# Attention and highway feed-forward on one core: later tail loads, a late last v load, turns ahead of stores

## The chip, the cores and the metric

The kernel runs on one core of one Trainium2 chip. The metric is the device time of one execution in microseconds, the median over several runs. Before the change three runs took 267.73, 270.59 and 270.0 us, so the median is 270.0 us.

## What is computed

For 8 batches of 12 heads, 448 rows and 64 columns, q and k are normalised row by row, the scores are divided by tau = 0.1, and softmax attention over v follows. The heads of a row are then laid side by side (768 numbers) and a highway layer closes the program.

```python
q_n = q / (np.linalg.norm(q, axis=-1, keepdims=True) + 1e-06)
k_n = k / (np.linalg.norm(k, axis=-1, keepdims=True) + 1e-06)
scores = np.matmul(q_n, k_n.transpose(0, 1, 3, 2)) / tau
attn = softmax(scores)
x = np.matmul(attn, v).transpose(0, 2, 1, 3).reshape(B * S, H * D)
H = np.maximum(x @ w_h, 0.0)
T = 1.0 / (1.0 + np.exp(-(x @ w_t + b_t)))
out = T * H + (1.0 - T) * x
```

## The kernel before

The 12 heads of a batch are worked as 6 pairs, so there are 48 pairs, numbered s = 6 b + p. Of the 448 rows of a head 384 form three full blocks of 128, and 64 are the tail. The main rows are loaded by POOL's queue, which turns float32 into float16 on the way: one transfer each for q, k and v of a batch (`ld6 qr b`, `ld6 kr b`, `ld6 vr b`, 576 KB, L342 and L365). The tails stay float32 and come on SP's queue, two transfers of 96 KB for each of q, k and v (`ldqt b h` at L357, `ldkt b ab` at L361, `ldvt b ab` at L367).

From the loads a batch goes through these steps:

- Squares of q and k, summed to norms: `sq3` for the main rows, `sqt b 0` for the q tail (ACT) and `sqt b 1` for the k tail (DVE or ACT), all through L258 or L264, then the folds (L421, L425, L427).
- Seven small DVE steps make the inverse roots (`nt84 b`, L465 to L471).
- The normalised main rows of a pair are written by `qn s` and `kn s` (L258) on DVE or POOL. The normalised tails of a whole batch are written into one buffer by `kb b 0`, `kb b 1` (k) and `qtn b` (q).
- Turning: for batches 4 to 7 SP issues a DMA transpose for each pair (`xd6 q s`, L572, tile qT) and one for the tails of a batch (`xd9 t b`, L599, tile tT). For batches 1 to 6 the rows x that attention leaves are also turned by two DMA transposes of SP (`xd12 b 0` and `xd9 b 1`, L757, tile xT).
- PE makes the scores of a pair in three groups `qk s c` (L642) and one for the tail keys `qkt s` (L657). ACT takes the exponential of each (`exp s c`, L648, and `expt s`, L661).
- PE multiplies with v (`av s c`, L690 and L694, `avt s`, L710), DVE divides by the sums (`rc s`, L718, and `ev s`, L720). v itself is copied beforehand into a buffer with columns of ones (`vc b p` and `vtc b ab`, L261).
- The highway layer of a batch is four groups g = 4 b + i. PE makes `fft`, `ffc` (L800, L807, L791), ACT a tanh (`th`, L848, L849), DVE the relu minus x (`hm`, L867), the gate (`gt`, L872; `gg`, L879) and, with POOL, the sum (`out`, L884). SP stores the rows (`st g` at L898, `sth g h` at L891).

Nothing schedules this at run time. The program is recorded as a list of 1717 operations, and the table `ORDER` gives the order in which they are emitted; every engine then runs its own operations strictly in that order, and a wait of one holds up all behind it. The table `SLOTS` gives, in the order of first use, which buffer of its ring each tile takes:

```python
def follow(self, order, slots):
    out, at = [], 0
    for n in order:
        o = self.ops[n]
        for t in self.new(o):
            self.slot[t] = slots[at]
            at += 1
        out.append(o)
```

The rings that matter here: qt, kt and vt have two buffers each, so batches 4 and 6 share one and 5 and 7 the other; vr has three, vp two; qT three (two pairs each), qn two (two pairs each); PSUM has three double banks `pS` for scores and highway products, and two single banks `pB`. The first highway product of group 13 (`fft4 13 0 0`) takes the bank of `qk 24 1`, so it cannot begin before `exp 24 1` has read it.

The edits touch operations 1303 to 1306 and 1310 (order of k, q and v tails of batch 6), 1505 to 1515 and 1540 to 1545 (those of batch 7 and what hangs on its v), and a few stores and turns, all of them by their place in the table alone.

Of the kernel before, what the change touches and what calls it, by code (L numbers as in the profile page):

```python
# [93 lines left out]
001000101001011010001001001101200002010102110111002010110010120120101112011200001100210200010111101211100200011  # L94
010121101110012010001110200001001021200211101012020101011010201110110121100211010001102011120112012121110000101
100021101121211010022102010100101020101012011210211201110120121001020201210110020012110220201001111102111010011
012001102000110023200021110200121101110010012110121010210102210000201001000112011010203210111001102010110021110
201210221101220100000001111210001102221120101021010210121001021011001110121001110123101211022001101020020100112
201101000120122101120201010102001010110220011012020001102010211111010202120100211120011122111012120012100110211
000200021110010011001010202112221011000010120001001101210001101010221101220201130110201020012020011110100221020  # L100
21032102101100121011102301000121210121010230201
""".replace("\n", "")
)
# [906 lines left out]
```

## Time and profile before

| what | us |
|---|---|
| median of three runs | 270.0 |
| lowest, highest run | 267.73, 270.59 |
| the profiled execution | 272.19 |
| its span, first to last instruction | 270.4 |
| PE busy in the span | 244.4 |
| DVE busy | 228.5 |
| ACT busy | 206.0 |
| POOL busy | 115.9 |

The profiled execution is 1.8 us longer than its span, and 2.2 us longer than the median. "PE" is TensorE, "SPq" the queue of SyncE on which DMAs are issued. In a timeline a row has its start, its length, engine, source line, operation and tiles; what stands in brackets is the idle time of that engine just before the row and what ended it. Rows of SP and DMA rows of POOL are issues: how long the transfer itself takes is told by its landing.

### The profile page before, as it was taken

The page shows a single profiled execution, that of the slowest core. Times are in us where ns is not written, and L with a number is a line of the kernel's source. Part 1 is how long each engine was busy: PE and PEld are TensorE (multiplying, and loading weights), DVE is VectorE, ACT ScalarE, POOL GpSimd, SP SyncE. Part 2 cuts the span into 40 slices and gives each one's busy share as a digit, 9 for nine tenths or more (in the row PEclk, how much of TensorE's full clock was granted, in tenths as well). Part 3 has the DMA queues.
Part 4 walks back from the last instruction along what each step waited for, and adds up shares of the span by engine and source line. Part 5 has one row for each costly group of instructions (what it writes and reads, how often), then busy time and mean ns, then how long its engine had stood idle before and what let it go on. Part 6 is the DMA issues. An engine that isn't in the chain of part 4 may idle for free.

```text
span 270.4 us, 9033 instructions
## 1 busy us (share of the span) xinstructions
PE 244.4 (90%) x3755; PEld 165.0 (61%) x3755; DVE 228.5 (85%) x513; ACT 206.0 (76%) x279; POOL 115.9 (43%) x151
## 2 busy tenths in 40 slices
PE   7088978999999999999899799997999999999991
PEld 3044666676776676667466557664767667767650
DVE  6599899999999898998976978997987864569894
ACT  3379999799999989989589499867868797961120
POOL 8757458563455649335450626314404522002140
PEclk9659999999999999999999799999999999999998
DMA  7999999999899797999999976999939949413133
GB/s 136 207 192 183 179 200 211 194 184 193 136 136 252 103 152 84 172 253 157 178 166 173 187 196 128 206 136 154 235 107 175 183 72 238 80 58 119 63 100 132
DMA packets 104025, 43.32 MB, mean 160 GB/s; under 512 B 97584, under 2 KB 101040, under 8 KB 103984
## 3 DMA queue, kind: packets, MB, share of 16 engines
q0 software_dynamic: 38608, 16.52, 49.1%
q1 hardware_dynamic: 63920, 25.50, 48.8%
q10 hardware_dynamic: 1456, 0.72, 1.0%
q8 instruction: 29, 0.48, 0.7%
q14 instruction: 12, 0.10, 0.1%
HBM read 38.21 MB, written 11.01 MB: 182 GB/s over the span
## 4 chain that ended last, share of the span: by engine, by line
PE 62%; DVE 20%; DMA 7%; issue 4%; ACT 3%; POOL 2%; SPq 1%; DVEq 0%; PEldq 0%; ACTq 0%; POOLq 0%
PE pS L807 26%; PE pS L642 9%; PE pB L694 8%; PE pS L791 4%; PE pB L710 4%; PE pB L657 3%; PE pB L690 3%; DMA kt<-in_k_dram 3%; DVE qn L258 3%; PE pB L582 2%; DMA qr<-in_q_dram 2%; DVE x L720 2%; DMA qT<-qn 2%; DVE f L421 2%; DVE hm L867 1%
## 5 line engine op out<-in xcount | busy, mean ns | idle before, releaser
L648 ACT ACTIVATE E<-pS 128x896 f16<-128x896 f32 x144 | 127.3, 924 | 26.2 <-PE pS L642 22.5
L807 PEld LDWEIGHTS <-xT 64*128 64x128 f16 x1128 | 53.8, 94 | 31.6 <-issue 2.6
L807 PE MATMUL pS<-wt,xT 64*128 64x384 f16 x576 | 56.6, 325 | 0.2 <-PEq L800 0.2
L807 PE MATMUL pS<-wh,xT 64*128 64x384 f16 x552 | 55.7, 323 | 0.2 <-DVE hm L867 0.2
L642 PE MATMUL pS<-qT 64*128 64x384 f16 x288 | 43.9, 332 | 2.3 <-DMA qT<-qn 1.8
L694 PE MATMUL pB<-vp,E 128*128 128x65 f16 x864 | 43.8, 194 | 0.0
L694 PEld LDWEIGHTS <-E 128*128 128x128 f16 x864 | 38.8, 98 | 2.6 <-issue 2.5
L867 DVE SCALAR_TENSOR_TENSOR hm<-pS,x 128x768 f16<-128x768 f32 (+1 forms) x33 | 27.3, 831 | 10.7 <-ACT tt L848 5.7
L642 PEld LDWEIGHTS <-qT 64*128 64x128 f16 x576 | 22.9, 95 | 19.6 <-issue 4.4
L690 PE MATMUL pB<-vp,Et 128*128 128x130 f16 x144 | 32.0, 222 | 2.3 <-DVE x L720 1.9
L258 POOL TENSOR_TENSOR qn<-kr,rs 128x384 f16<-128x384 f16 x24 | 19.8, 827 | 32.9 <-issue 10.0
L884 POOL TENSOR_TENSOR os<-x,hm 128x768 f32<-128x768 f16 (+1 forms) x11 | 15.8, 1441 | 37.7 <-DVE hm L879 17.3
L720 DVE SCALAR_TENSOR_TENSOR x<-pB,rd 128x448 f16<-128x448 f32 x48 | 29.7, 621 | 1.1
L661 ACT ACTIVATE Et<-pB 128x512 f16<-128x512 f32 x48 | 28.9, 609 | 0.9 <-PE pB L657 0.8
L642 PE MATMUL pS<-tT,qT 64*128 64x64 f16 x282 | 27.6, 190 | 0.0
L258 POOL TENSOR_TENSOR qn<-qr,rs 128x384 f16<-128x384 f16 x17 | 14.4, 850 | 14.0 <-DMA qT<-qn 5.6
L884 DVE TENSOR_TENSOR os<-x,hm 128x768 f32<-128x768 f16 (+1 forms) x22 | 18.5, 842 | 0.8 <-POOL os L884 0.6
L845 ACT ACTIVATE tt<-os 128x768 f16<-128x768 f32 (+1 forms) x8 | 6.1, 764 | 17.1 <-DVE os L839 10.0
L710 PE MATMUL pB<-vp,E 128*128 128x65 f16 x288 | 18.6, 195 | 0.5 <-POOL vp L261 0.5
L258 DVE TENSOR_TENSOR qn<-qr,rs 128x384 f16<-128x384 f16 x30 | 17.2, 577 | 0.5 <-POOL qn L258 0.4
L690 PEld LDWEIGHTS <-Et 128*128 128x128 f16 x144 | 14.1, 98 | 5.5 <-issue 4.3
L879 DVE TENSOR_TENSOR hm<-tt,hm 128x768 f16<-128x768 f16 (+1 forms) x33 | 16.4, 503 | 0.4
(116 smaller groups left out, 451.2 us busy)
## 6 DMA issues: line engine op xcount, KB each, us to landing
out_dram<-os SPq DMA_DIRECT2D x23, 384.0 KB, 3.0
vr<-in_v_dram POOLq DMA_DIRECT2D x8, 576.0 KB, 11.3
kr<-in_k_dram POOLq DMA_DIRECT2D x7, 576.0 KB, 10.8
qr<-in_q_dram POOLq DMA_DIRECT2D x7, 576.0 KB, 10.7
qt<-in_q_dram SPq DMA_DIRECT2D x16, 96.0 KB, 5.4
vt<-in_v_dram SPq DMA_DIRECT2D x16, 96.0 KB, 5.6
out_dram<-os SPq DMA_DIRECT2D x15, 96.0 KB, 2.7
kt<-in_k_dram SPq DMA_DIRECT2D x14, 96.0 KB, 6.7
```

Source lines behind the costliest of these rows:

```text
L258: return (nc.vector if eng == "DVE" else nc.gpsimd).tensor_mul(out_, a, c)
L642: ins = nc.tensor.matmul(dst, lhsT=qT[ln, 384 + 128 * c : 512 + 128 * c], rhs=rhs, start=True, stop=True)
L648: return nc.scalar.activation(R("E", s)[:, c, :, 0:448], R("S", 3 * s + c)[:, :, 0:448], AF.Exp, scale=inv_tau)
L661: op("ACT", f"expt {s}", lambda: nc.scalar.activation(R("Et", s)[:, 64:576], R("B", ("S", s))[:, :], AF.Exp, scale=inv_tau), key + 3, r=[( ...
L690: nc.tensor.matmul(U[:, 2 * c : 2 * c + 2, :].rearrange("p g e -> p (g e)"), lhsT=Et[:, 128 + 128 * c : 256 + 128 * c], rhs=vp[:, 6:8, :]. ...
L694: ins = nc.tensor.matmul(U[:, 2 * c + ab, :], lhsT=EF[:, j, 576 * ab + 128 * c : 576 * ab + 128 * c + 128], rhs=vp[:, 3 * ab + j, :], star ...
L710: ins = nc.tensor.matmul(U[:, 6, :], lhsT=lt, rhs=rh, start=(n == 0), stop=(n == 7))
L720: op("DVE", f"ev {s}", lambda: nc.vector.scalar_tensor_tensor(out=R("x", b)[:, :, D * p : D * p + D], in0=U_()[:, :, 0:D], scalar=0.0, in1 ...
L807: ins = nc.tensor.matmul(P[:, h, 0:MH], lhsT=lt, rhs=rh, start=(part == 0 and cc == (-1 if wi == 0 and not added else 0)), stop=(part == 1 ...
L867: return nc.vector.scalar_tensor_tensor(out=o_, in0=i0, scalar=0.0, in1=xs, op0=ALU.max, op1=ALU.subtract)
L879: op("DVE", f"gg{'h' if tail or last_ else ''} {nm}", lambda cs=cs: nc.vector.tensor_mul(R("hm", g)[:, cs], R("tt", g)[:, cs], R("hm", g)[ ...
L884: op(en, f"out{'h' if tail or last_ else ''} {nm}", lambda eng=eng, cs=cs: eng.tensor_add(R("os", g)[:, cs], xall()[:, cs], R("hm", g)[:, ...
```

## The change

Only the two tables change. On SP the k tails of batch 6 move up to where one of the q tails of batch 6 was, and the q tails move down to where the k tails were; the tails of batch 7 and the v tails of batch 6 are gathered at other places; three DMA transposes move ahead of stores. On POOL the v load of batch 7 moves down by some 25 operations. The v copies of batch 7 move with it, and the v buffers of batches 6 and 7 trade places.

```diff
-814 783 483 994 838 484 836 839 834 659 1123 837 974 805 1303 804 787 1310 835 803 976 802 788 660 934 806 832
-817 807 661 833 1029 935 662 818 474 819 663 843 1304 841 820 842 1114 840 1311 485 823 937 824 475 821 650 822
...
+814 783 483 994 838 484 836 839 834 659 1123 837 974 805 804 787 1310 835 803 976 802 788 660 934 806 832 817
+807 661 833 1029 935 1306 1305 662 818 474 819 663 843 841 820 842 1114 840 1311 485 823 937 824 475 821 650
```

First place, SP, the turns of pairs 26 and 27 and of the tails of batch 4. Here qt_76 and kt_78 are the buffers of batches 4 and 6, qt_77 and kt_79 those of 5 and 7; qT_107 is turned from the pairs 27 and 26, tT_103 from the tails of batch 4.

```order
 L357 DMA qt_77<-in_q_dram 64x6x64
-L572 DMA_TRANSPOSE qT_107<-qn_101 128x6x128
-L357 DMA qt_76<-in_q_dram 64x6x64
-L572 DMA_TRANSPOSE qT_107<-qn_101 128x6x128
+L572 DMA_TRANSPOSE qT_107<-qn_101 128x6x128 x2
 L599 DMA_TRANSPOSE tT_103<-kb_80 128x9x128
-L357 DMA qt_76<-in_q_dram 64x6x64
+L361 DMA kt_78<-in_k_dram 64x6x64 x2
 L891 DMA out_dram<-os_130 64x384
 L898 DMA out_dram<-os_128 128x768
```

One q load no longer stands ahead of the turn of the tails; both k loads of batch 6 stand right behind it.

Second place, SP, some ten issues later, behind the turns of pairs 29 and 28 (qT_106).

```order
 L757 DMA_TRANSPOSE xT_120<-x_116 128x12x128
 L572 DMA_TRANSPOSE qT_106<-qn_102 128x6x128 x2
+L357 DMA qt_76<-in_q_dram 64x6x64 x2
 L891 DMA out_dram<-os_129 64x384
-L361 DMA kt_78<-in_k_dram 64x6x64 x2
 L757 DMA_TRANSPOSE xT_119<-x_116 128x9x128
```

Where the k tails of batch 6 were issued, one store earlier, its q tails are issued now.

Third place, SP, the end of batch 4's highway layer and the first turns of batch 6 (tT_103, qT_105; vt_85 and vt_86 are the v tails of batches 6 and 7).

```order
 L757 DMA_TRANSPOSE xT_119<-x_117 128x9x128
-L367 DMA vt_85<-in_v_dram 64x6x64
+L367 DMA vt_86<-in_v_dram 64x6x64 x2
+L367 DMA vt_85<-in_v_dram 64x6x64 x2
 L599 DMA_TRANSPOSE tT_103<-kb_80 128x9x128
 L572 DMA_TRANSPOSE qT_105<-qn_102 128x6x128 x2
+L572 DMA_TRANSPOSE qT_107<-qn_101 128x6x128 x2
 L898 DMA out_dram<-os_128 128x768
-L367 DMA vt_85<-in_v_dram 64x6x64
 L898 DMA out_dram<-os_129 128x768
```

Four v tail loads instead of one now stand ahead of the turn of the tails of batch 6, and two turns ahead of two stores.

POOL, two pieces. The first is the group of three main loads of batch 7; the second is where its v load (vr_82 now) stands, behind the first v copies of batch 6.

```order
 L342 DMA qr_71<-in_q_dram 128x12x192
-L365 DMA vr_83<-in_v_dram 128x12x192
 L342 DMA kr_74<-in_k_dram 128x12x192
...
 L421 TENSOR_TENSOR f_93<-sq_91 128x384
-L261 COPY vp_88<-vr_82 128x6x64 x2
-L261 CAST vp_88<-vt_85 64x6x64
+L261 COPY vp_87<-vr_83 128x6x64 x2
+L365 DMA vr_82<-in_v_dram 128x12x192
+L261 CAST vp_87<-vt_85 64x6x64
```

The load leaves the middle of the group and is issued right after two copies of batch 6. ACT keeps its order here but for one v copy, and so does PE altogether.

More of the change, by code (lines that the diff above doesn't have):

```diff
@@ L96 @@
 100021101121211010022102010100101020101012011210211201110120121001020201210110020012110220201001111102111010011
[L97 to L100, printed above, removed]
+012001102000110023200021110200121101110010012110121010210102210000201001000112011010203210111011020100110021110
+201210221101202010000001111200011022211201010210102101210010210110011110121001110230121102200110102002010012201
+101001201212101120201010101200101111022001101202000110201021111101020212010021112000101221110121200121001102110
+002000211100100110010101202112221011000010120001001101210001101010212101220201130110201020012020011110100221020
 21032102101100121011102301000121210121010230201
```

54 rows, old and new, of the table ORDER are left out of this document.

## The prediction

> **What bounds the kernel now.** I read the page first, then PE's waits in order of time, then the stretch around the longest of them.
>
> ```profile
> PE 244.4 (90%) x3755; PEld 165.0 (61%) x3755; DVE 228.5 (85%) x513; ACT 206.0 (76%) x279; POOL 115.9 (43%) x151
> PE 62%; DVE 20%; DMA 7%; issue 4%; ACT 3%; POOL 2%; SPq 1%; DVEq 0%; PEldq 0%; ACTq 0%; POOLq 0%
> ```
>
> PE sets the end: it is busy for 90% of the span and has 62% of the chain that ended last. The change first moves an instruction at about 125 us. In PE's timeline behind that point only three waits are longer than 0.3 us:
>
> ```profile
> 131.95 0.20 PE L657 MATMUL pB<-tT 128*128 128x64 f16 x1 [1.13 <-DMA tT<-kb]
> ...
> 150.78 0.22 PE L690 MATMUL pB<-vp,Et 128*128 128x130 f16 x1 [1.89 <-DVE x L720]
> ...
> 188.80 0.34 PE L642 MATMUL pS<-qT 64*128 64x384 f16 x2 [1.76 <-DMA qT<-qn]
> ```
>
> Together 4.8 us: more can't be won from waits. What stands behind the middle one is told by the chain in order of time and by DVE's timeline:
>
> ```profile
> 137.63 0.68 SPq L361
> 138.36 8.51 DMA kt<-in_k_dram
> 146.96 0.56 DVE sq L258
> ```
>
> ```profile
> 146.96 0.56 DVE L258 TENSOR_TENSOR sq<-kt 128x384 f16<-128x384 f32 x1 [2.31 <-DMA kt<-in_k_dram]
> ...
> 148.32 0.20 DVE L718 RECIPROCAL rd<-pB 128x7 f32<-128x7 f32 x1
> ...
> 150.12 0.61 DVE L720 SCALAR_TENSOR_TENSOR x<-pB,rd 128x448 f16<-128x448 f32 x1
> ...
> 158.81 0.63 DVE L872 TENSOR_SCALAR tt<-tt 128x768 f16<-128x768 f16 x2 [1.37 <-ACT tt L849]
> ```
>
> The k tails of batch 6 take 8.5 us to land, DVE stands 2.31 us before squaring them, and `rc 24` and `ev 24` queue behind; PE waits for `ev 24`, which ends at 150.73. The granted clock follows:
>
> ```profile
> 148.70:152.10 3.40, 1.51 (x40) 1.42 (x39) 3.40 (x7) 0.95 (x3) 1.43 (x2) 1.00 1.46 195
> 152.10:155.60 3.50, 3.50 (x43) 2.34 (x41) 3.47 (x8) 2.40 (x3) 2.76 (x4) 0.51 1.31 175
> ```
>
> The 3.5 us after the stretch with the long wait ran at 0.51 of the clock.
>
> **The change part by part**, against the profiled execution (272.19 us, span 270.4), which is 2.2 us over the median of the three runs.
>
> *1. The turn of batch 4's tails goes out earlier.* SP's timeline before:
>
> ```profile
> 125.05 0.60 SPq L357 DMA_DIRECT2D qt<-in_q_dram  x1
> 125.75 1.26 SPq L572 DMA_TRANSPOSE qT<-qn  x1
> 127.14 1.29 SPq L599 DMA_TRANSPOSE tT<-kb  x1
> 128.47 0.60 SPq L357 DMA_DIRECT2D qt<-in_q_dram  x1
> 129.12 1.61 SPq L891 DMA_DIRECT2D out_dram<-os  x1
> ...
> 131.66 0.53 SPq L891 DMA_DIRECT2D out_dram<-os  x1
> 132.30 1.40 SPq L757 DMA_TRANSPOSE xT<-x  x1
> 133.79 3.15 SPq L572 DMA_TRANSPOSE qT<-qn  x2
> 137.00 0.58 SPq L891 DMA_DIRECT2D out_dram<-os  x1
> ```
>
> The load at 125.05 leaves (0.70 with its gap), so the turn is issued at 126.4, and 96 KB fewer lie ahead of it. PE's 1.13 us for tT shrink by 0.70 at least; I take all 1.13, since the transfer ahead goes too. Bounds 0.7 and 1.13.
>
> *2. The k tails of batch 6* go out behind that turn, near 127.8 and 128.4; at the 8.5 us of the slow case they land by 137, long before DVE asks at 144.65. DVE's 2.31 us go, `ev 24` no longer holds PE: 1.89 us. Next late would be `av 24`, whose exponentials ACT makes (part 4).
>
> *3. The half clock.* At full rate the 3.5 us would have taken 3.5 x 0.51 = 1.8, so up to 1.7 us return if PE alone sets the pace there. DVE is nearly as full (3.47 of 3.50), but it will be 2.3 us ahead and stands 1.37 us idle at 158.81. I take 1.3, bounds 0 and 1.7. The waits of 1.13 and 1.76 us were followed by no such dip. The Trainium skill, "TensorE: Matmul & The Clock Gate", section "Why this matters for your kernels", has the clock fall only after gaps of more than about 3 us; by that this dip hangs on something else and stays, and the sum would be 1.3 us worse. Here 1.89 us came before one.
>
> *4. The q tails of batch 6 go where the k tails were, and ACT needs them sooner than DVE needed those.*
>
> ```profile
> 139.97 0.53 ACT L264 ACTIVATE sq<-qt 128x384 f16<-128x384 f32 x1
> 140.38 0.92 ACT L648 ACTIVATE E<-pS 128x896 f16<-128x896 f32 x1
> ...
> 141.59 0.33 PE L807 MATMUL pS<-bth,ones 64*128 64x384 f16 x2
> ```
>
> ACT squares qt at 139.97. Right behind it is `exp 24 1`, and the product at 141.59 takes that very bank, so a late qt stops ACT and 1.6 us later PE. When are they issued? At the latest 137.0 and 137.65, behind the two turns that end at 136.94. At the earliest 134.9 and 135.5: of the store at 129.12 (1.61) 1.05 are more than its like takes (0.53, 0.58), and 0.5 lie empty around 131; both stand beside the slow tT turn, and with the 0.6 of part 1 SP could be 2.1 us ahead. POOL's big load starts between the two:
>
> ```profile
> 136.29 1.09 POOL L342 DMA_DIRECT2D qr<-in_q_dram  x1
> 137.37 1.01 POOL L365 DMA_DIRECT2D vr<-in_v_dram  x1
> ```
>
> Times to landing of three issues on SP (qt at 125.05, no POOL load beside it; vt at 173.67, 0.07 ahead of one; the store at 137.00, 0.71 behind one):
>
> ```profile
> DMA to landing us min/median/max: 2.7/2.7/2.7
> ...
> DMA to landing us min/median/max: 3.8/3.8/3.8
> ...
> DMA to landing us min/median/max: 4.3/4.3/4.3
> ```
>
> So the second half lands between 138.2 (135.5 + 2.7) and 146.2 (137.65 + 8.5). Nearest is the load issued as a POOL load starts: 135.5 + 3.8 = 139.3. With PE 1.13 ahead, ACT would ask at 138.84: 0.5 us lost. Bounds 0 and 6.
>
> *5. Four v tail loads ahead of the turn of batch 6's tails*, beside v of batch 6:
>
> ```profile
> 173.67 0.63 SPq L367 DMA_DIRECT2D vt<-in_v_dram  x1
> 179.43 1.28 SPq L599 DMA_TRANSPOSE tT<-kb  x1
> 180.81 5.33 SPq L572 DMA_TRANSPOSE qT<-qn  x2
> ```
>
> ```profile
> 173.74 1.08 POOL L365 DMA_DIRECT2D vr<-in_v_dram  x1
> ```
>
> At 0.65 each the last goes out near 175.7 and lands 3.8 to 8.5 later, 179.5 to 184.2; the turn at 179.43 comes out of the ring behind it, 0 to 4.8 us later. SP's empty time (174.30 to 179.43) covers most: I take 0.7. Below nothing, at most the 1.76 us wait at 188.80 can go, if the slow turns at 180.81 happen to be quicker.
>
> *6. v of batch 7* leaves the stretch from 137 us on and is issued behind the two copies at 191.29, at 192.2, next to the turn of x of batch 5:
>
> ```profile
> 191.29 0.95 POOL L261 COPY vp<-vr 128x384 f16<-128x384 f16 x2
> ```
>
> ```profile
> 193.59 1.31 SPq L757 DMA_TRANSPOSE xT<-x  x1
> ```
>
> ```profile
> 198.81 0.33 PE L807 MATMUL pS<-bth,ones 64*128 64x384 f16 x2
> ```
>
> That turn landed 3.9 us later, at 197.5, and PE uses it at 198.81. Without the v tail load ahead it is issued at 192.9. The turn at 180.81 beside v of batch 6 took 7.3, the one at 139.94 in the traffic of three POOL loads 11.2:
>
> ```profile
> DMA to landing us min/median/max: 7.3/7.3/7.3
> ...
> DMA to landing us min/median/max: 11.2/11.2/11.2
> ```
>
> 192.9 + 7.3 = 200.2: PE waits 1.4. Bounds 0 (3.9) and 5.3 (11.2).
>
> The rest costs nothing: the moved v copies take 0.3 to 0.8 us each in idle time of their engines, the tails of batch 7 land 10 us before use, and the turns ahead of stores are 0.6 us earlier for tiles that PE does not wait for.
>
> **Sum**: -1.13 - 1.89 - 1.3 + 0.5 + 0.7 + 1.4 = -1.7. 272.19 - 1.7 = 270.5 for the profiled execution, 268.3 against the median.
>
> **The rivals.**
>
> *ACT waits for qt* (slower). If SP is not ahead and the load falls under POOL's, the second half lands at 143.7 (137.65 + 6, between 3.8 and 8.5). `exp 24 1` then ends 1.3 later, PE resumes near 145.0 instead of 141.59: 3.4 late; it reaches the place of 150.78 at 148.9 + 3.4 = 152.3, 1.5 later than before, with the dip still there. With parts 5 and 6: +3.6, 273.6. From a landing at 142.1 on, the stage loses what parts 1 and 2 win. For it: 8.5 us for the very loads that stood in this place. Against it: vr no longer follows, the store ahead is now behind, and SP may be early.
>
> *Turns starve* (slower). Parts 5 and 6 at 3 us each: -3.8 + 6.0 = +2.2, 272.2. For it: 11.2 us for a turn under load; against it: only one POOL load runs at each place.
>
> *The dip stays*, for a reason other than the wait: idle stretches of 1.13 and 1.76 us had none, so 1.89 us need not be its cause. -1.7 + 1.3 = -0.4, 269.6. The Trainium skill's rule of part 3 would have it so; that the dip comes 1.4 us behind the longest wait speaks against it.
>
> *Hidden anyway*: what is won by 156 us is spent before 200 us, since DVE at 85% and the turns wait in the same order as before: 270.0.
>
> **How the numbers follow.** Forecast 0.45, ACT waits 0.2, turns starve 0.12, dip stays 0.13, hidden 0.1. The forecast's own range, from part 5 won (-1.76) to part 6 at 3: 265.8 to 270.0. The range of all, leaving out the far ends of ACT's wait, is 265.0 to 273.0. About 1% (2.7 us) is what a measurement of this kernel can tell from no change. Faster by more (under 267.3): 0.27, nearly all from the forecast with part 5 or 6 at its low end. Slower by more (over 272.7): 0.2, from the two slower rivals. Within 1%: 0.53.
>
> **What would show it.** Right: no wait of DVE for kt near 145 us, no PE wait near 131 and 149, no half clock near 152, ACT's `sq<-qt` with less than 1 us idle ahead, PE's longest new wait on xT near 199. Wrong: ACT idle several us before `sq<-qt` and PE idle right after; tT or qT of batch 6 landing after 190; the half clock at the same place without a wait ahead of it.

## The result and the profile after

The changed kernel takes 285.0 us (median of four executions, 282.4 to 286.3) against 270.3 us for the kernel before on the same chip: a ratio of 1.054, 95% interval 1.049 to 1.060. The forecast was 268.3 us with a range up to 273.0, so the change went the other way. The profiled execution took 284.71 us with a span of 282.9, 12.5 us more than the 270.4 of before.

The first lines of the page, as shown of before, already say what kind of loss it is:

```profile
PE 247.6 (88%) x3755; PEld 166.4 (59%) x3755; DVE 229.8 (81%) x513; ACT 206.0 (73%) x279; POOL 115.5 (41%) x151
PE 57%; DVE 20%; DMA 11%; issue 4%; ACT 3%; POOL 2%; SPq 0%; DVEq 0%; ACTq 0%; PEldq 0%; POOLq 0%
```

The work of the engines is nearly the same (PE 244.4 us before), but transfers have gone from 7% to 11% of the chain that ended last. PE's timeline gives the places; each row has its partner among the rows of before, and the difference of the starts is what has been lost up to there:

```profile
131.09 0.20 PE L657 MATMUL pB<-tT 128*128 128x64 f16 x1
...
147.40 0.51 PE L807 MATMUL pS<-bth,ones 64*128 64x384 f16 x2 [6.50 <-ACT E L648]
...
156.87 0.22 PE L690 MATMUL pB<-vp,Et 128*128 128x130 f16 x1
...
194.72 0.34 PE L642 MATMUL pS<-qT 64*128 64x384 f16 x2 [3.03 <-DMA qT<-qn]
...
204.94 0.34 PE L807 MATMUL pS<-bth,ones 64*128 64x384 f16 x2 [0.24 <-DVE hm L867]
209.53 2.10 PE L807 MATMUL pS<-wt,xT 64*128 64x384 f16 x12 [4.25 <-DMA xT<-x]
```

The rows of before stood at 131.95, 141.59, 150.78, 188.80 and 198.81, and the last one at 198.97 (a row not shown). So: 0.86 us won at the tails of batch 4; 5.81 lost at the first product of group 13; 6.09 lost at `av 25`; 5.92 and 6.13 lost at the next two, so hardly more there; 10.56 lost at the x turn of batch 5; 12.5 at the end. Two events, 6.7 us near 146 and 4.4 near 207, and 1.9 behind the second.

**The first event.** All engines' rows between 136 and 147 us:

```profile
136.63 1.09 POOL L342 DMA_DIRECT2D qr<-in_q_dram  x1
137.14 1.37 SPq L357 DMA_DIRECT2D qt<-in_q_dram  x2
137.71 1.02 POOL L342 DMA_DIRECT2D kr<-in_k_dram  x1
...
146.02 0.52 ACT L264 ACTIVATE sq<-qt 128x384 f16<-128x384 f32 x1 [6.79 <-DMA qt<-in_q_dram]
```

and the two loads seen by themselves:

```profile
DMA to landing us min/median/max: 6.1/7.1/8.1
```

The q tails of batch 6 are issued 0.51 us behind POOL's load of q of batch 7. They land 6.1 and 8.1 us after their issue, ACT stands 6.79 us before `sqt 6 0`, `exp 24 1` behind it keeps its bank, and PE stands 6.50 us for that bank.

**The second event.** All engines' rows around 200 us, and the turn by itself:

```profile
197.76 1.09 POOL L365 DMA_DIRECT2D vr<-in_v_dram  x1
...
201.17 4.48 SPq L757 DMA_TRANSPOSE xT<-x  x1
```

```profile
DMA to landing us min/median/max: 8.3/8.3/8.3
```

The turn of x of batch 5 goes out 3.4 us behind POOL's load of v of batch 7, takes 4.48 us to issue (1.31 before) and 8.3 to land (3.9 before).

**The clock.** The windows in which the granted clock was halved (columns: length, then busy time of PE, PEld, DVE, ACT, POOL, the granted clock, the DMA share, GB/s):

```profile
145.50:152.40 6.90, 5.00 (x36) 2.84 (x37) 2.73 (x9) 3.84 (x6) 0.82 (x1) 0.51 0.91 114
...
206.95:213.80 6.85, 4.27 (x30) 2.12 (x32) 2.18 (x6) 0.00 (x0) 2.44 (x3) 0.50 1.12 236
```

The dip of before at 152 is gone, and each of the two long waits has one of twice its length around its end.

In what follows one execution of c1, the profiled one, and one of the kernel before beside it ran at nearly twice the time from start to end; no reading rests on them.

### The profile page after: what moved, and what is told of

Read it like the earlier page. It is cut to its first block, busy times and chain, and to the rows that moved or that the text cites. A ratio compares the mean times of both kernels' runs of the same rounds, so it can differ in the third digit from the quotient of the medians.

```text
span 282.9 us, 9040 instructions
## 1 busy us (share of the span) xinstructions
PE 247.6 (88%) x3755; PEld 166.4 (59%) x3755; DVE 229.8 (81%) x513; ACT 206.0 (73%) x279; POOL 115.5 (41%) x151
## 4 chain that ended last, share of the span: by engine, by line
PE 57%; DVE 20%; DMA 11%; issue 4%; ACT 3%; POOL 2%; SPq 0%; DVEq 0%; ACTq 0%; PEldq 0%; POOLq 0%
PE pS L807 26%; PE pS L642 8%; PE pB L694 7%; PE pB L710 3%; PE pB L657 3%; DMA xT<-x 3%; PE pS L791 3%; DMA qt<-in_q_dram 3%; PE pB L690 3%; DVE qn L258 3%; PE pB L582 2%; DMA qr<-in_q_dram 2%; DVE os L884 2%; DVE x L720 2%; DMA qT<-qn 2%
## 5 line engine op out<-in xcount | busy, mean ns | idle before, releaser
L807 PEld LDWEIGHTS <-xT 64*128 64x128 f16 x1128 | 55.0, 96 | 37.3 <-DMA xT<-x 4.5
L807 PE MATMUL pS<-wt,xT 64*128 64x384 f16 x576 | 59.5, 337 | 4.4 <-DMA xT<-x 4.3
L807 PE MATMUL pS<-wh,xT 64*128 64x384 f16 x552 | 56.3, 325 | 0.2 <-DVE hm L867 0.2
L258 POOL TENSOR_TENSOR kb<-kt,rs 64x384 f16<-64x384 f32 x9 | 7.4, 822 | 27.6 <-DVE tt L872 10.6
L718 DVE RECIPROCAL rd<-pB 128x7 f32<-128x7 f32 x48 | 9.4, 198 | 10.5 <-PE pB L694 6.9
```

The source lines that it names most:

```text
L258: return (nc.vector if eng == "DVE" else nc.gpsimd).tensor_mul(out_, a, c)
L718: op("DVE", f"rc {s}", lambda: nc.vector.reciprocal(R("rd", s)[:, :], U_()[:, :, D]), key + 1, r=[("B", ("U", s))], w=[("rd", s)])
L807: ins = nc.tensor.matmul(P[:, h, 0:MH], lhsT=lt, rhs=rh, start=(part == 0 and cc == (-1 if wi == 0 and not added else 0)), stop=(part == 1 ...
```

## The experiments

No kernel leaves work out. The diffs show rows of SP and POOL; where v of batch 7 moves, its copies on the other engines and the buffers of v move with it. In the diffs qt_76 and kt_78 are the q and k tail buffers of batch 6, vt_86 those of the v tails of batch 7, vr_82 or vr_83 v of batch 7, xT_119 and xT_120 the turns of x. Times are medians with lowest and highest. Where the executions of one kernel spread widely, I give the range and not the ratio.

### One part undone at a time

**u1**, the q and k tails put back:

```diff
-L361 DMA kt_78<-in_k_dram 64x6x64 x2
+L357 DMA qt_76<-in_q_dram 64x6x64
...
-L357 DMA qt_76<-in_q_dram 64x6x64 x2
 L891 DMA out_dram<-os_129 64x384
+L361 DMA kt_78<-in_k_dram 64x6x64 x2
```

> The changed kernel with the q and k tails of batch 6 back at their places of before; all else as changed. Theory: the late landing of qt 6 (8 us beside POOL's loads of q and k of batch 7) stops ACT 6.8 us, PE 6.5 us, and brings the half clock of 6.8 us behind it; with the tails back ACT's wait for qt and PE's wait of 6.5 us near 146 go, DVE's wait for kt near 145 is back (smaller than 2.31 us if the third POOL load, v of batch 7, is what made it so long), and at group 14 the kernel stands 4.7 us better than the changed one: 280.3 us, 278.0 to 281.0. The later waits, 3.0 us on qT near 190 and 4.3 us on xT near 207 with its half clock, stay. Rival: the time is set by what comes later (the turns behind 180 us) and the stretch at 146 is absorbed: 284 to 286 us.

Measured 281.3 us (277.8 to 282.4); the kernel before on this chip 270.4. PE's rows of the profile:

```profile
152.34 0.22 PE L690 MATMUL pB<-vp,Et 128*128 128x130 f16 x1 [2.26 <-DVE x L720]
...
206.47 1.78 PE L807 MATMUL pS<-wt,xT 64*128 64x384 f16 x10 [6.40 <-DMA xT<-x]
```

The wait at 146 is gone and PE's wait behind DVE is back, as expected. DVE's share of it for kt is only 1.02 us here; ahead of that it stands 1.62 us for a store (see b1). The time is 0.3 us above the expected range; in the profile the second event has grown, to 6.40 us from 4.25. It did not need the first.

**u2**, v of batch 7 and its copies put back (the v tails stay gathered):

```diff
 L342 DMA qr_71<-in_q_dram 128x12x192
+L365 DMA vr_83<-in_v_dram 128x12x192
 L342 DMA kr_74<-in_k_dram 128x12x192
...
-L365 DMA vr_82<-in_v_dram 128x12x192
```

> The changed kernel with the main load of v of batch 7 and its copies back at their places of before; the tails of v stay early, the stores stay moved. Theory: that load, issued by POOL next to the turn of x of batch 5, makes the turn land 12 us later than before, PE stands 4.3 us for xT and then runs 6.8 us at half clock; with the load back PE's wait for xT is under 1 us and 5.1 + 1.6 = 6.7 us return: 278.3 us. But three loads of POOL then stand beside the q tails of batch 6 again, which may land up to 2 us later: 277.5 to 281. Rival: the stores that were moved in front of that turn hold it up: then the turn still lands late, PE still waits about 4 us for xT and the time stays at 284 to 286 us (or more, by the later q tails).

Measured 277.6 us (273.0 to 279.6). The x turn lands 4.4 us after its issue and PE does not wait for it: the rival falls. The profile is of the 273.0 us execution and shows something not asked for:

```profile
138.37 1.38 SPq L357 DMA_DIRECT2D qt<-in_q_dram  x2
139.12 1.09 POOL L342 DMA_DIRECT2D qr<-in_q_dram  x1
```

```profile
DMA to landing us min/median/max: 2.5/3.1/3.7
```

Here SP's q tails were issued ahead of POOL's load, by 0.75 and 0.02 us, and landed in 2.5 and 3.7 us. ACT did not wait for them. So the median of u2 is not the price of the late v alone.

**u3**, two stores put back ahead of the turns of pairs 39 and 38:

```diff
-L572 DMA_TRANSPOSE qT_107<-qn_101 128x6x128 x2
 L898 DMA out_dram<-os_128 128x768
 L898 DMA out_dram<-os_129 128x768
+L572 DMA_TRANSPOSE qT_107<-qn_101 128x6x128 x2
```

> The changed kernel with two stores of the highway layer (groups 13 and 14) back ahead of a turn, as before, all else as changed. Theory: the stores do not make the x turn of batch 5 late, the POOL load beside it does: PE still waits about 4.3 us for xT near 207 and the time stays within 1 us of the changed kernel, 284 to 286. Rival: these stores, issued 1 to 3 us ahead of the turn and in flight beside it, hold it up: the wait falls to under 1 us and the time to 278.5 us.

Measured 285.2 us (277.8 to 286.2). The x turn is as late as in the changed kernel, so the moved stores are not what holds it up:

```profile
197.07 1.09 POOL L365 DMA_DIRECT2D vr<-in_v_dram  x1
...
199.08 5.39 SPq L757 DMA_TRANSPOSE xT<-x  x1
...
210.45 1.78 PE L807 MATMUL pS<-wt,xT 64*128 64x384 f16 x10 [5.82 <-DMA xT<-x]
```

**u4**, three of the four v tail loads put back:

```diff
+L367 DMA vt_86<-in_v_dram 64x6x64
 L757 DMA_TRANSPOSE xT_120<-x_117 128x12x128
+L367 DMA vt_86<-in_v_dram 64x6x64
...
-L367 DMA vt_86<-in_v_dram 64x6x64 x2
-L367 DMA vt_85<-in_v_dram 64x6x64 x2
+L367 DMA vt_85<-in_v_dram 64x6x64
...
+L367 DMA vt_85<-in_v_dram 64x6x64
```

> The changed kernel with three of the four loads of v tails (both of batch 7, one of batch 6) back at their places of before, so that one instead of four stands ahead of the turns of batch 6 near 180 us. Theory: the four loads beside the POOL load of v of batch 6 make those turns land late; with three away PE's wait on qT falls from 3.0 us to about 1.8, as before, and the time falls by 1.3: 283.7 us. Rival: the turn is late because of the POOL load alone, or the wait is taken up again by the xT wait behind it: 285.0 us, no change.

Measured 280.4 us (277.8 to 284.4), below both expectations. PE's wait on qT did fall, to 0.93 us; the turn of the tails of batch 6 lands in 6.2 us instead of 9.1. But in the profiled execution SP's q tails were again ahead of POOL's load, by 1.26 us, and ACT did not wait, while PE's wait for xT grew to 7.08 us: the median is not the price of the v tails alone. Inconclusive on the size.

### One part done alone

**b3**, only the q and k order of the change in the kernel before:

```diff
-L357 DMA qt_76<-in_q_dram 64x6x64
+L361 DMA kt_78<-in_k_dram 64x6x64 x2
...
+L357 DMA qt_76<-in_q_dram 64x6x64 x2
 L891 DMA out_dram<-os_129 64x384
-L361 DMA kt_78<-in_k_dram 64x6x64 x2
```

> The kernel before with only the q and k tails of batch 6 at their places of the changed kernel. Theory: the race of SP and POOL decides. Where the q tails are issued behind POOL's load of q of batch 7 (by 0.5 us in the changed kernel) they land 8 us later, ACT and PE stand over 6 us and a half clock follows: 4.7 us worse, 275 us, 274 to 277. In an execution in which POOL's load comes later than they do, ACT does not wait: 267 us. Rival: the wait is taken up by slack behind it: 269.5 to 271.

Measured 273.9 us (271.4 to 274.3), ratio 1.014 (1.005 to 1.022): a little slower, on the low edge of what was expected. The profile is one in which SP was ahead, by 1.01 and 0.28 us; the tails landed in 2.5 and 2.9 us and ACT did not wait, as the theory has it. But for such an execution 267 us were expected and this one took 273.8: there the theory missed. Its profile has two other waits of PE, 2.06 us at 115.24 for the x turn of batch 2, which lies ahead of every edit, and 2.25 us at 189.17 for qT, each with a half clock of 3.41 us. So the 3.3 us of b3 over before are not the price of the late q tails.

**b2**, only v of batch 7 late, in the kernel before:

```diff
-L365 DMA vr_83<-in_v_dram 128x12x192
...
 L261 COPY vp_87<-vr_83 128x6x64 x2
+L365 DMA vr_82<-in_v_dram 128x12x192
+L261 CAST vp_87<-vt_85 64x6x64
```

> The kernel before with only the main load of v of batch 7 and its copies at their places of the changed kernel; no store and no tail load moved. Theory: the load beside the turn of x of batch 5 is enough by itself: that turn lands 8 to 12 us after its issue instead of 3.9, PE waits 4 to 7 us for xT near 205 and has a half clock behind it; +7 to +9 us: 278 us, 276.5 to 280. Rival: the load hurts only together with the moved stores or the gathered v tails: 269.5 to 272.

Measured 274.0 us (270.8 to 279.9), 3.3 above before where 7 to 9 were expected. The late turn is there without any other part. The profile is of an execution of 271.4 us, in which PE waited less than expected and no half clock followed; the two longer ones, 276.6 and 279.9 us, have no profile:

```profile
187.10 1.09 POOL L365 DMA_DIRECT2D vr<-in_v_dram  x1
189.60 4.74 SPq L757 DMA_TRANSPOSE xT<-x  x1
...
198.11 1.15 PE L807 MATMUL pS<-wt,xT 64*128 64x384 f16 x12 [2.38 <-DMA xT<-x]
```

**b1**, all four q and k tails early, in the kernel before:

```diff
 L599 DMA_TRANSPOSE tT_103<-kb_80 128x9x128
-L357 DMA qt_76<-in_q_dram 64x6x64
+L361 DMA kt_78<-in_k_dram 64x6x64 x2
+L357 DMA qt_76<-in_q_dram 64x6x64 x2
...
-L361 DMA kt_78<-in_k_dram 64x6x64 x2
```

> The kernel before with one thing changed: all four q and k tail loads of batch 6 stand right behind the turn of batch 4's tails on SP, about 7 us ahead of POOL's loads. Theory: the waits of before for tT (1.13 us) and behind kt (1.89 us, with the half clock that follows it) go and no wait of ACT for qt comes in their place, so the part of the change that is good in itself is worth up to 4.4 us: 266.0 us, 265.0 to 267.5. Rival: what is won near 150 us is spent again by the turns behind 180 us, which wait in the same order as before: 269.5 to 270.5.

Measured 272.3 us (268.2 to 275.2), ratio 1.001 (0.994 to 1.008): no gain, the theory missed. The wait at 150 is still there with kt long landed:

```profile
136.59 1.09 POOL L342 DMA_DIRECT2D qr<-in_q_dram  x1
...
138.75 1.38 SPq L891 DMA_DIRECT2D out_dram<-os  x1
...
146.60 0.96 DVE L884 TENSOR_TENSOR os<-x,hm 128x768 f32<-128x768 f16 x1 [2.66 <-issue]
...
151.78 0.22 PE L690 MATMUL pB<-vp,Et 128*128 128x130 f16 x1 [2.20 <-DVE x L720]
```

The store at 138.75, 2.2 us behind POOL's load, took 7.8 us and landed at 146.53; DVE's `out 10` writes the very buffer that it reads and began at 146.60. The profile of b1 names no releaser there; the buffer numbers and the two times do, and u1's profile names a store of os in front of the same row, with 1.62 us.

**c3** takes that store, and the one before it, out of the way:

```diff
+L891 DMA out_dram<-os_129 64x384 x2
 L361 DMA kt_79<-in_k_dram 64x6x64
...
+L361 DMA kt_78<-in_k_dram 64x6x64 x2
+L357 DMA qt_76<-in_q_dram 64x6x64 x2
...
-L891 DMA out_dram<-os_129 64x384
```

> The kernel before with all four q and k tail loads of batch 6 right behind the turn of batch 4's tails, and the two stores of group 3's tail rows issued some 15 us earlier, so that neither loads nor those stores are issued behind POOL's loads of batch 7. Theory: the early tails alone gained nothing because the store of group 3, issued 1.1 us behind POOL's load, took 7.8 us to land and stopped DVE 2.66 us before it could write that buffer; with the store out of the way the waits of before near 131 and 150 us go and nothing takes their place: 267.5 us, 266 to 269. Rival: what is won is spent again further on: 269.5 to 271.5.

Measured 271.1 us (268.5 to 272.9), ratio 1.002 (0.997 to 1.006). The wait at 150 is gone, so the store was its cause in b1; but the time does not move, and the rival holds. In its profile PE waits 1.29 us for tT though no q load of batch 6 stands ahead of that turn, and 2.13 us at 115.66 for the x turn of batch 2, which is issued ahead of every edit and made PE wait neither in the profile of before nor in that of the changed kernel.

### The two faults mended or undone together

**b4**, the changed kernel with its q tails right behind its k tails:

```diff
 L361 DMA kt_78<-in_k_dram 64x6x64 x2
+L357 DMA qt_76<-in_q_dram 64x6x64 x2
...
-L357 DMA qt_76<-in_q_dram 64x6x64 x2
 L891 DMA out_dram<-os_129 64x384
```

> The changed kernel with its q tails of batch 6 issued right behind its k tails, 8 us earlier, all else as changed. Theory: ACT's wait of 6.8 us, PE's of 6.5 and the half clock behind it go and what was won ahead of them stays: 4.7 + 4.4 = 9 us less, 276 us, 275 to 279; PE's waits on qT near 190 and xT near 207 stay or grow, since PE comes to them earlier. Rival: the loads wait for something else than POOL's load (the buffers, or the places in the queue), and ACT stands again at qt: 284 to 286.

Measured 278.8 us (275.7 to 282.3), as expected. No wait for qt; waits of 2.58 us for qT at 186.67 and 2.96 for xT at 201.20 are left. The buffers were free and SP had room, so the place of the loads was what made them late.

**c2**, both parts put back (the diffs of u1 and u2 together):

> The changed kernel with both of its costly parts put back: the q and k tails of batch 6 and the load of v of batch 7 with its copies at their places of before. What is left of the change are the gathered v tails, the stores, the turns ahead of stores and the tails of batch 7. Theory: the two parts are the whole loss but for 0 to 1.5 us of the v tails: 271.2 us, 270 to 273. Rival: the rest holds part of the loss, since each part undone alone left 280 to 281 and 277.6: 275 to 279.

Measured 272.2 us (270.4 to 273.8), ratio 1.009 (1.005 to 1.013). The two parts hold all but about 2 of the 14.7 us.

**c4**, the diffs of b4 and u2 and the early stores of c3, in the changed kernel:

> The changed kernel with the load of v of batch 7 and its copies at their places of before, the q tails of batch 6 right behind its k tails, and the two stores of group 3's tail rows some 15 us earlier. Theory: no transfer that an engine waits for is issued behind a POOL load but the turns of batch 6, with the gathered v tails ahead of them (+1.3): 269 us, 267 to 271. Rival: the gathered tails, stores and turns of the change cost more than that by themselves: 272 to 277.

Measured 272.5 us (271.5 to 275.5), ratio 1.011 (1.005 to 1.018): above the theory's range. Part of it is of my making. The copy of the v tail of batch 7 was put back early while its load stayed late, and DVE shows it:

```profile
184.81 0.36 DVE L261 CAST vp<-vt 64x384 f16<-64x384 f32 x1 [3.90 <-DMA vt<-in_v_dram]
```

Behind it PE stands 3.63 us for DVE. The same copy waits 2.05 us in u2 and not at all in the profile of c2. So part of what c4 leaves is not the change's; c2, 1.6 us above before in the medians, is the better measure of the rest.

**c1 and d3** (one kernel, run twice), the changed kernel with one row of POOL moved by one place:

```diff
 L261 COPY vp_87<-vr_83 128x6x64 x2
+L261 CAST vp_87<-vt_85 64x6x64
 L365 DMA vr_82<-in_v_dram 128x12x192
-L261 CAST vp_87<-vt_85 64x6x64
```

> The changed kernel with one instruction of POOL one place later: the load of v of batch 7 behind the copy of the v tail of batch 6 instead of ahead of it, which puts it about 1.5 us behind the issue of the x turn of batch 5 instead of 3 us ahead. Theory: first come, first served: a transfer of SP issued ahead of POOL's load lands in 4 to 5 us, one behind it in 8 to 12; the x turn lands in time, PE's wait for xT goes to under 1.5 us and the time falls by 4 to 7: 280 us, 278 to 281 (the wait for qt near 146 stays). Rival: the load slows any turn in flight beside it, ahead or behind: xT still lands 8 us after its issue and the time stays at 284 to 286.

c1: 276.0 us over twelve executions; eleven lie between 269.3 and 280.4. Below the expectation, and four of them under 272.

> The kernel c1 again (the changed kernel with POOL's load of v of batch 7 one instruction later), for a profile: the profiled execution of c1 ran at 511 us as a whole and can't be read. Theory: xd12 of batch 5, issued ahead of POOL's load, lands in 4 to 6 us, and PE's wait for xT near 205 is under 1.5 us; what is left is the wait for qt near 146 in the executions in which SP comes second: 269 to 272 without it, 276 to 280 with it. Rival: xT still lands 8 us or more after its issue, and the good times of c1 come from elsewhere.

d3: 274.9 us (271.5 to 282.8): three executions at 271.5 to 272.8, three at 277.0 to 282.8. The profile, of one of the latter:

```profile
138.31 1.37 SPq L357 DMA_DIRECT2D qt<-in_q_dram  x2
138.63 1.09 POOL L342 DMA_DIRECT2D qr<-in_q_dram  x1
145.46 0.52 ACT L264 ACTIVATE sq<-qt 128x384 f16<-128x384 f32 x1 [4.23 <-DMA qt<-in_q_dram]
...
198.88 1.79 SPq L757 DMA_TRANSPOSE xT<-x  x1
200.98 1.09 POOL L365 DMA_DIRECT2D vr<-in_v_dram  x1
```

The x turn is now 2.1 us ahead of POOL's load and lands in 3.8 us; PE does not wait for it. The second event is gone with one row moved by one place. The first is there by halves: of the q tails one was issued 0.3 us ahead of POOL's load, the other 0.4 behind, and ACT waited 4.23.

**d2**, the changed kernel once more:

> The changed kernel itself, unchanged, for the spread of its executions and a second profile. Theory: which queue comes first is decided in each execution by what went before (in six traces in which the x turn of batch 2 landed 7 to 7.6 us after its issue instead of 4.5, POOL came later and SP's tails were ahead). So the times fall in two groups: most at 282 to 286 with ACT waiting 6 to 7 us for qt, and a few at 276 to 279 without that wait; the wait for xT near 207 is in both. The profile shows the wait for qt if and only if the q tails are issued behind POOL's load of q. Rival: the spread is something else, and the wait of ACT does not follow that order.

Measured 286.7 us (280.6 to 289.5). Not two clean groups. The profile again splits the two halves of the q load:

```profile
140.22 1.37 SPq L357 DMA_DIRECT2D qt<-in_q_dram  x2
140.61 1.09 POOL L342 DMA_DIRECT2D qr<-in_q_dram  x1
...
147.40 0.52 ACT L264 ACTIVATE sq<-qt 128x384 f16<-128x384 f32 x1 [4.20 <-DMA qt<-in_q_dram]
```

The first half, 0.39 us ahead, landed after 2.6 us, the second, 0.34 behind, after 6.4. So in this profile the wait does follow the order; that the groups blur because the order can fall between the halves fits it, but the other executions have no profile.

**d1**, the moves of b4 and of c1 together, all else as changed:

> The changed kernel with two small moves: its q tails of batch 6 right behind its k tails on SP (8 us ahead of POOL's load instead of 0.5 us behind it), and POOL's load of v of batch 7 one instruction later (behind the issue of the x turn of batch 5 instead of ahead of it). Nothing else is put back; v of batch 7 stays late. Theory: in the traces so far a tail load issued ahead of POOL's load, if only by 0.02 us, landed in 2.5 to 3.9 us, one issued 0.35 us or more behind it in 5.2 to 9.4; which of the two comes first is the whole of both faults, so both go: no wait of ACT for qt, PE's wait for xT near 200 under 1.5 us, and what is left of the change costs 0 to 3: 272 us, 270 to 274, in one cluster. Rival: the late load of v costs by being late, wherever it stands: 276 to 280.

Measured 272.0 us (five executions from 270.0 to 273.5, one at 280.3; before 270.3), beside 286.7 for the changed kernel on the same chip.

```profile
130.38 1.66 SPq L357 DMA_DIRECT2D qt<-in_q_dram  x2
...
138.19 1.09 POOL L342 DMA_DIRECT2D qr<-in_q_dram  x1
...
192.62 2.38 SPq L757 DMA_TRANSPOSE xT<-x  x1
...
194.90 1.09 POOL L365 DMA_DIRECT2D vr<-in_v_dram  x1
```

Neither ACT's wait for qt nor PE's for xT is left (2.60 us for qT are), with v of batch 7 still late and the v tails still gathered. The one high execution has no profile. No version here beats the kernel before by more than the measurement can tell.

## Why the prediction was wrong, point by point

**Part 4 failed, on the step that took SP to be early and so to issue the q tails ahead of POOL's load.** It put the q tails of batch 6 at 134.9 and 135.5 at the earliest and 137.0 and 137.65 at the latest, and took the early end, because a store of 1.61 us and 0.5 us of empty time looked like slack that the slow turn had caused. With the turn quick (3.0 us instead of 4.8) SP still issued them at 137.1 and 137.9, past the late end. The slack was not there. The store took 1.40 us all the same; the empty half microsecond before the next store stands in eleven of the sixteen readable profiles, slow turn or not; and the 0.6 us of the q load that left ahead of the turn were spent behind it, where two k loads took the place of one q load, so that this store went out at 129.44 instead of 129.12. From there my own upper bound held: 137.65 + 8.5 = 146.2, and the last half landed at 145.9. The term was 0.5 us and measured 6.7 at the first product of group 13. The rival "ACT waits" had the mechanism but a landing at 143.7, the middle of its own bounds, so its price was too small as well. b4 and d1 show the cause: the same loads, some 7 us earlier, and the wait is gone.

What I did not see is that the outcome hangs on an order, and that the order differs between executions. In the seven profiles with the q tails in their changed place, the two in which the x turn of batch 2 landed in 4.6 us had SP behind POOL; in the five in which it took 7.3 to 7.7 PE was held up near 115, POOL's load came later, and SP's first half was ahead.

**Part 6 failed in its size: the landing time of the x turn of batch 5.** The term was 1.4 us, with 7.3 for the turn taken from a turn near one POOL load. Measured are 4.4 us of wait and about 1.9 behind it. Two of its numbers were short. The turn's landing: with POOL's v load 2.0 to 3.4 us ahead it took 8.3 to 11.6 us in seven profiles; in the seven with that load elsewhere 3.8 to 5.0, and in the two with it 2.1 to 2.3 behind 3.8 and 4.4. And its issue: forecast 0.7 us earlier than before, it came 7.6 later (201.17 against 193.59) where PE was 6.13 late, since SP was busy almost without a break with the turns and stores ahead of it. The bound (11.2 us) was right; the value was not.

**Part 3 was half right.** The old dip is gone, worth about 1.4 us (the stretch from `av 25` to PE's wait for qT took 0.17 us less than before with a wait 1.27 us longer at its end). That the wait brought the dip is not shown: b1 and u1 have waits of 2.20 and 2.26 us at the same place and no dip behind them, so the term may have come out by luck. And the same rule of thumb should have priced the new waits: I put the half clock of new waits at nothing, and two of 6.83 us came. c2, d1 and b1, without long waits, have no dip of that length.

**Part 1 was right in the number and wrong in the reason.** PE came 0.86 us earlier to the tails of batch 4. But tT lands 4.6 and 5.0 us after its issue in b1 and c3, which have no q load ahead of it, and 3.0 in b2, which has one: the load was not what made it slow, and what did is open. That the number came out is luck.

**Part 2 was right.** With the k tails early DVE does not wait for kt in the changed kernel, b4 or d1.

**Part 5 was right within its bounds.** Forecast 0.7 us (-1.76 to 4.8), measured 1.27 us more of PE's wait on qT (3.03 instead of 1.76). The turn of the tails of batch 6 lands in 8.4 to 9.3 us in eight of the ten profiles with four v tail loads ahead of it (6.9 and 7.8 in the others) and in 5.7 to 7.6 in the six with one.

**What the sum of 1 to 3 was worth.** b1 and c3 were to show 4.4 us by themselves and show none (c3: -0.7 us to +1.6). The "hidden" rival describes it. b1's gain went to a store; where c3's went is not settled, beyond the 1.29 us for tT and the 2.13 for the x turn of batch 2.

**How the parts add up.** The whole change costs 14.7 us. In the changed kernel, mending the first fault alone leaves 278.8 us (b4), the second alone 275 to 276 (c1, d3), both 272.0 (d1). Done alone in the kernel before, each part costs 3.3 us in the medians, but b3's profile does not hold the wait for qt, and b2's is of one of its quick executions, so these are not the prices of the two faults. Whether one wait makes the other worse was not tried apart.

## What to carry to other kernels

Where two queues share the transfer engines (the page gives both as shares of the same 16), ask of each small transfer that an engine waits for on which side of the other queue's large load it is issued: here a tail load 0.3 to 1 us behind it landed in 5.2 to 8.8 us, one up to 2 us ahead of it in 2.5 to 3.9 but for one. Price such a transfer by the late end of its issue time, and if the order can fall either way, move it well clear or swap it with a neighbour; for the x turn of batch 5 one place was enough. And when a load is delayed to "when its buffer is free", list what will be issued right behind it in its new place.

## What the runs showed of the hardware

**The landing goes with the order of issue.** From the starts and landings of SP's transfers in the sixteen readable profiles (worked out from their timelines, from 95 us on), against POOL's nearest 576 KB load, or the first of them where two or three follow each other:

| SP's transfer | issued | count | landing, us |
|---|---|---|---|
| tail load, 96 KB | 0 to 2 us ahead | 24 | 2.5 to 3.9, one 6.3 |
| tail load | up to 0.1 behind | 2 | 3.4 and 4.0 |
| tail load | 0.3 to 1 behind | 11 | 5.2 to 8.8 |
| tail load | 1 to 5 behind | 75 | 6.5 to 9.7 |
| turn of x of batch 2 | 0.8 ahead | 16 | 4.4 to 4.7 (6), 7.0 to 7.7 (10) |

A turn seems to need more lead than a load: at 0.8 us ahead it goes either way, and when it goes wrong PE waits 1.5 to 2.2 us near 115, in variants of both kernels; the x turn of batch 5, 2.1 to 2.3 us ahead, landed in 3.8 and 4.4. The Trainium skill, "DMA: Bandwidth & Descriptors", section "Queues, rings and completion order", says that each transfer engine takes turns between the queues packet by packet. By that, if the turns were of equal length, a tail load beside one other queue would take at most about twice its 2.7 us, 5.4 as an estimate; the runs show up to 9.7, so turns of equal length alone do not explain them. The packets in the trace of the changed kernel show more (first 138.2 to 139.4 us, then 147 to 149; q0 is POOL's queue, q1 SP's; packets, MB, share):

```profile
q0 software_dynamic: 82, 0.03, 57.8%
...
q0 software_dynamic: 556, 0.21, 85.1%
q1 hardware_dynamic: 556, 0.14, 53.9%
```

In the second stretch the two queues move the same number of packets, which agrees with turns. In the first, 1.6 us and more behind the issue of POOL's load, SP's queue moves nothing, though both q loads had been issued at 137.14 and 137.87. What holds them there is not shown.

**The half clock.** From 60 us on, waits of PE of 4.25 us and more (seven) had a half clock of 6.83 us or longer around their end. Of those between 1.5 and 4 us some had one, mostly of 3.41 us, and some none, and their length does not tell which: 1.87 us had one, 3.90 had none. All such stretches were 3.41 us long or a multiple, but for the last of each profile, which runs into its end. The rule of the Trainium skill that I weighed in part 3 ("TensorE: Matmul & The Clock Gate", section "Why this matters for your kernels"), a gap of more than about 3 us, agrees with the long waits and not with the short ones that had a half clock, nor with 3.90 that had none.
